# Chunked attention and a top-2 expert layer in one kernel: a new schedule for the attention, with its first loads, transposes and routing moved

## The chip, the cores and the metric

The kernel runs on one core of a Trainium2 chip. The number that counts is the device time of one execution in microseconds, the median of three runs. The core has five engines that each work through their own instructions in order: PE (matrix multiplications and transposes by matrix multiplication), DVE (vector), ACT (scalar and activation), POOL (GpSimd) and SP, which here only issues transfers. They wait for each other with semaphores. Transfers run on 16 DMA engines that all queues share. The profile is one execution recorded by the hardware.

## The reference

Two layers, the second fed by the first. The attention has 4 batches, 8 heads, 768 positions, head size 64. Positions are cut into chunks of 32; a chunk sees 16 positions before it, itself, 8 after it, and 8 memory rows.

```
scores = scale * q_c @ concat(mem_k, k_ctx).T
a      = softmax(scores)
out_c  = a @ concat(mem_v, v_ctx)
```

Its output, 3072 rows of 512, goes through a mixture of 8 experts (512 to 1024 to 512). Each row takes the two experts with the largest noisy gate values:

```
noisy  = x @ w_gate + log1p(exp(x @ w_noise)) * noise
top2   = the two largest, weights = softmax over the two
out    = sum over the two of  weight * (relu(x @ w1[e]) @ w2[e])
```

## The kernel before

**Attention.** A tile is 256 positions of one batch, so there are three tiles a batch and twelve in all, counted by `i`; `tp` is the tile within its batch. The main loop (L538) works on several tiles at once. In iteration `i` the scores of tile `i+1` are computed (`scores`: PE into PSUM, then a maximum and a subtraction on DVE), the exponentials of tile `i` are turned (`turn_p`: eight PE transposes, an ACT copy), `values` multiplies them with v and scales by the reciprocal sums, and tile `i-1` is sent to DRAM (`keep_x`, on SP, into `xd`), turned (`turn_x`: eight PE transposes and an ACT copy, L465 and L467) and multiplied with the gate weights (`gate`). `exps` is the exponential on ACT and comes near the end of the iteration.

**Input units.** k, q and v of a batch are loaded by POOL with a cast to bf16 (`load`, L112; 1.5 MB of fp32 each), into four buffers `nat`. Each is cut into three parts: a unit is one part. `mix` (L350) brings a part into an order in which it can be turned, `turn` (L366) transposes it with eight PE transposes into PSUM, `settle` (L375) copies it into `kT`, `qT` or `vT`, two copies for k and one for q and v. The nine units of a batch are spread over earlier iterations by `groups`. For batch 0 DVE does the first six mixes and shares the copies with ACT; after that POOL mixes and ACT copies.

**Spans of v.** `windows` turns `vT` back into rows for each chunk, 16 small PE transposes and one DVE copy (L386) for each half of a tile; `memory_rows` (L391) then adds the memory rows with two transfers from SP.

**Routing.** `Route` picks the two experts of the 768 rows of a batch, as a code for one of 28 pairs: noise on ACT, `choose` on DVE (the last step builds `ohp`, a 0/1 mask of rows by pairs, L255), `ranks` (place of a row within its pair, on PE), `weights` (L271 to L276), `place`, `total` (running counts, L293 and L297), `slots` (a one-hot of the rank, L303), `values` of the route (L308, POOL) and `lists` (L315, PE), which adds to `listed`, a table with the rows of each pair. Routing of a batch is spread over the iterations of the next one, by the `yield`s of `route`. The last batch is routed after the loop, in two portions.

**PSUM.** Most transposes share a ring of three buffers (`psT`); the gate's result shares one buffer with the sums of `values` (tag `ps_g`, L438 and L474).

**Experts.** Rows are gathered by pair from `xd` (`gathers`, POOL), the first six pairs by PE and the rest by DMA transposes on SP (L663), and worked through in 20 steps of one expert and two to four pairs. `load_expert` brings w1 and w2 of one expert with a cast, 2 MB as bf16, from POOL; experts 0, 1, 2 and 3 are loaded at the ends of iterations 3, 4, 6 and 8, expert 4 behind the second gathers, the others by `feed` during the steps. A pair is scattered to the output with `put` (L644, POOL) when its second expert is done; the pairs done in the last two steps are held in `held`.

**End.** If a pair has too many rows for the tables, a branch (L940) works on the rest; with this data it is not taken. The held scatters stand behind the branch in the text, but POOL's order is set by a scheduler there, which brings all but one of them ahead of it.

The order on PE, ACT, DVE and SP in the attention is written out by hand (`manual_schedule`). POOL's is set by a scheduler, with `pin` keeping mixes, loads, gathers and scatters in their order. The attention's buffers are cut from the end of `w_all`, the array of the expert weights (`scratch`), down into expert 3; experts 0 to 2 are free of them.

Of the kernel before, what the change touches and what calls it, by code (L numbers as in the profile page):

```python
# [22 lines left out]
def kernel(  # L23
# [82 lines left out]
    assert scol[0] // WE >= 3  # L106
    stage = xrow[1].rearrange("p s r -> p (s r)").bitcast(F32)

# [5 lines left out]
    for n in range(4):  # L114
        load(n)
# [14 lines left out]
    mks = stage[:, 0:2 * D].rearrange("p (x d) -> p x d", x=2)  # L130
    nc.sync.dma_start(out=mks, in_=mem_k.rearrange("b h m d -> (b h m) d").rearrange("(x p) d -> p x d", p=128))
    mkn = keep.tile([128, 2, D], BF16, name="mkn")
    nc.vector.tensor_copy(mkn, mks)
    mvs = stage[0:B * NM, 2 * D:2 * D + Dm].rearrange("p (h d) -> p h d", h=H)
    for b in range(B):
        nc.sync.dma_start(out=mvs[b * NM:(b + 1) * NM], in_=mem_v[b].rearrange("h m d -> m h d"))
    mvn = keep.tile([B * NM, Dm], BF16, name="mvn")
    nc.vector.tensor_copy(mvn.rearrange("m (c g d) -> m c g d", c=HP, g=2), mvs.rearrange("m (g c) d -> m c g d", g=2))
    wgs = stage[:, 2 * D + Dm:2 * D + Dm + KP * 2 * E].rearrange("p (k e) -> p k e", k=KP)
    nc.scalar.dma_start(out=wgs[:, :, 0:E], in_=moe_w_gate.rearrange("(kp p) e -> p kp e", p=128))  # L140
    nc.scalar.dma_start(out=wgs[:, :, E:2 * E], in_=moe_w_noise.rearrange("(kp p) e -> p kp e", p=128))
    wgn = const.tile([128, KP, 2 * E], BF16, name="wgn")
    nc.vector.tensor_copy(wgn, wgs)
# [46 lines left out]
    for i in range(2):  # L190
        nc.vector.memset(kT[i], 0.0)
    nc.vector.memset(vT[:, :, 0:LC], 0.0)
    nc.vector.memset(vT[:, :, LC + S:VP], 0.0)

# [12 lines left out]
    class Route:  # L207
# [23 lines left out]
        def choose(self):  # L231
# [23 lines left out]
            nc.vector.tensor_tensor(out=self.M, in0=pcode.unsqueeze(1).to_broadcast([128, n, NP]), in1=bc(pc[:, 0], NP), op=Alu.is_equal)  # L255
# [34 lines left out]

        def total(self):
# [8 lines left out]
        def slots(self, eng):  # L300
            n = self.n
            self.oh_l = work.tile([128, n, 128], BF16, name="oh_l")
            eng.tensor_tensor(out=self.oh_l, in0=bc(self.rr, 128), in1=io_l.unsqueeze(1).to_broadcast([128, n, 128]), op=Alu.is_equal)  # L303

# [18 lines left out]
    def route(b):  # L323
        r = Route(b * SO, SO, lgs[b])
        r.noise()
        yield
        advance(r.choose())
        yield
        r.ranks()
        r.weights(nc.vector)  # L330
        advance(r.place())
        advance(r.total())
        yield
        r.values(nc.gpsimd, 0, NV)
        r.slots(nc.vector)
# [3 lines left out]

    groups = [[(3 * b + x, part) for x, part in g] for b in range(B)
              for g in ([(0, 0), (0, 1), (1, 0)], [(0, 2), (1, 1), (1, 2)], [(2, 0), (2, 1), (2, 2)])]
# [11 lines left out]
    def mix_group(g):  # L355
        if g < 3 * B:
            for n, part in groups[g]:
                mix(n, part, nc.gpsimd)
            for n in ((), (g - 1, g), (g,))[g % 3]:
                load(n + 4)  # L360
# [627 lines left out]
```

## Time and profile before

| | us |
|---|---|
| median of three runs | 367.88 (366.38 to 369.55) |
| the profiled execution | 370.21 |
| its span, first to last instruction | 368.6 |
| PE busy | 289.4 (79%) |
| DVE busy | 175.4 (48%) |
| ACT busy | 144.9 (39%) |
| POOL busy | 131.6 (36%) |
| mean granted clock of PE | 0.913 |

The shares are averages over two stages: the attention and routing until about 154 us, and the experts after it. A row of the grouped lines has the line, engine and operation, what is written and read, the count, then busy time and mean ns of one, and the idle time of the engine just before with what ended it. A row of the timeline has start, length, engine, line and, in brackets, the idle time before it and what ended that. A row of the windows has the stretch, its length, the busy time of PE, weight loads, DVE, ACT and POOL, then the clock, the share of the DMA engines and GB/s. SPq and POOLq are the issuing sides of SP and POOL.

### The profile page before, as it was taken

How to read it: one execution, taken by the hardware profiler on the slowest of the kernel's cores; microseconds unless marked ns; L12 is line 12 of the kernel's file. 1: busy time of each engine (PE TensorE's matmuls, PEld its weight loads, DVE VectorE, ACT ScalarE, POOL GpSimd, SP SyncE). 2: the span in 40 equal slices, each digit the busy share in tenths (PEclk: the TensorE clock that was granted, in tenths of full speed). 3: DMA queues.
4: the chain of work that ended last, by engine and by line, in shares of the span. 5: the costliest groups of instructions: out<-in, count | busy, mean ns of one | idle time of the engine just before them, and what ended most of it. 6: DMA issues, size and time to landing. Idle time of an engine off the chain costs nothing.

```text
span 368.6 us, 8521 instructions
## 1 busy us (share of the span) xinstructions
PE 289.4 (79%) x3636; PEld 191.0 (52%) x3636; DVE 175.4 (48%) x408; ACT 144.9 (39%) x202; POOL 131.6 (36%) x173
## 2 busy tenths in 40 slices
PE   0476777667747451589999999999989999999970
PEld 0465667657646331465554445764436676555530
DVE  6963565896896978421133300974300233311330
ACT  1448768669843331034333144222234212334200
POOL 6279354453030023744275440162480032201131
PEclk9988788899898855599999999999999999999996
DMA  7999979997969020376999999821189982100020
GB/s 125 213 213 196 192 136 203 217 190 140 164 112 215 18 67 25 88 139 124 194 199 255 182 226 85 119 98 49 66 150 188 205 173 79 51 2 3 21 96 28
DMA packets 44156, 48.33 MB, mean 131 GB/s; under 512 B 19367, under 2 KB 33447, under 8 KB 44112
## 3 DMA queue, kind: packets, MB, share of 16 engines
q0 software_dynamic: 22672, 40.51, 57.5%
q1 hardware_dynamic: 17296, 7.08, 10.5%
q10 hardware_dynamic: 4144, 0.13, 0.8%
q8 instruction: 30, 0.49, 0.5%
q14 instruction: 14, 0.11, 0.1%
HBM read 64.88 MB, written 10.55 MB: 205 GB/s over the span
## 4 chain that ended last, share of the span: by engine, by line
PE 26%; issue 20%; DMA 6%; POOL 5%; DVE 5%; another core or an unknown queue 2%; POOLq 1%
PE p_y L690 12%; PE p_h L681 12%; DMA out_dram<-y,main_dst 5%; POOL out_dram L644 3%; POOL xt L638 2%; DVE w_all L455 1%; DMA xt<-xd,main_src 1%; DVE oh_l L303 1%; PE p_list L315 0%; PE p_xt L658 0%; POOL w_all L815 0%; POOLq L983 0%; DVE cum L297 0%; POOL w_all L816 0%
## 5 line engine op out<-in xcount | busy, mean ns | idle before, releaser
L681 PE MATMUL p_h<-xTt,w_all 128*128 128x256 bf16 (+3 forms) x672 | 102.9, 313 | 1.4 <-issue 1.0
L690 PE MATMUL p_y<-w_all,h 128*128 128x512 bf16 x448 | 100.1, 379 | 1.4 <-ACT y L694 1.4
L681 PEld LDWEIGHTS <-w_all 128*128 128x128 bf16 x672 | 65.9, 101 | 36.6 <-issue 2.0
L669 ACT ACTIVATE h<-p_h 128x512 bf16<-128x512 f32 (+1 forms) x79 | 43.4, 550 | 94.0 <-PE p_h L681 85.5
L690 PEld LDWEIGHTS <-h 128*128 128x128 bf16 x448 | 43.7, 98 | 51.7 <-issue 1.7
L644 POOL DMA_INDIRECT out_dram<-y,main_dst x28 | 31.0, 1108 | 105.9 <-DVE y L696 78.7
L667 DVE TENSOR_SCALAR h<-p_h 128x512 bf16<-128x512 f32 (+1 forms) x47 | 29.5, 630 | 80.6 <-PE p_h L681 66.7
L350 POOL COPY w_all<-w_all 128x1024 bf16<-128x1024 bf16 x30 | 30.5, 1043 | 27.3 <-PE p_t L366 21.8
L696 DVE SCALAR_TENSOR_TENSOR y<-p_y,main_w,y 128x512 f32<-128x512 f32 x28 | 21.0, 750 | 39.0 <-PE p_y L690 35.7
L638 POOL DMA_INDIRECT xt<-xd,main_src x28 | 27.2, 973 | 22.2 <-DMA xTt<-xt 8.8
L366 PE MATMUL p_t<-identb,w_all 128*128 128x128 bf16 x288 | 24.8, 243 | 13.2 <-DVE w_all L350 7.6
L694 ACT ACTIVATE y<-p_y,main_w 128x512 f32<-128x512 f32 x28 | 19.2, 688 | 38.2 <-PE p_y L690 34.8
L366 PEld LDWEIGHTS <-w_all 128*128 128x128 bf16 x288 | 20.4, 111 | 14.9 <-DVE w_all L350 8.0
L375 ACT COPY kT<-p_t 64x1024 bf16<-64x1024 bf16 x21 | 21.1, 1007 | 12.9 <-DVE kT L375 11.1
L383 PE MATMUL p_v<-identb,w_all 128*64 128x128 bf16 x384 | 18.5, 252 | 7.4 <-ACT w_all L375 4.8
L308 POOL TENSOR_TENSOR vals<-ohp,facts 128x1008 bf16<-128x1008 bf16 (+2 forms) x5 | 6.6, 1312 | 39.9 <-DVE facts L276 39.9
L433 ACT COPY pT<-p_p 128x1024 bf16<-128x1024 bf16 x12 | 12.1, 1010 | 20.1 <-PE p_p L430 20.1
L383 PEld LDWEIGHTS <-w_all 128*64 128x64 bf16 x384 | 14.7, 128 | 10.2 <-ACT w_all L375 5.4
L467 ACT COPY xT<-p_x 128x1024 bf16<-128x1024 bf16 x12 | 12.1, 1012 | 15.6 <-PE p_x L465 15.6
L455 DVE TENSOR_TENSOR w_all<-ps_o,rs 128x512 bf16<-128x512 f32 x24 | 15.5, 687 | 5.4 <-PE ps_o L447 3.1
L386 DVE COPY w_all<-p_v 128x1024 bf16<-128x1024 bf16 x24 | 16.0, 683 | 3.0 <-PE p_v L383 3.0
L418 DVE TENSOR_TENSOR sc<-ps_s,mx 128x1024 f32<-128x1024 f32 x12 | 14.7, 1225 | 4.1 <-ACT pb L423 3.3
(177 smaller groups left out, 283.2 us busy)
## 6 DMA issues: line engine op xcount, KB each, us to landing
w_all<-in_moe_w_dram POOLq DMA_DIRECT2D x16, 1024.0 KB
w_all<-in_moe_w_dram POOLq DMA_DIRECT2D x8, 512.0 KB
w_all<-in_k_dram POOLq DMA_DIRECT2D x4, 768.0 KB
w_all<-in_q_dram POOLq DMA_DIRECT2D x4, 768.0 KB
w_all<-in_v_dram POOLq DMA_DIRECT2D x4, 768.0 KB
xd<-w_all SPq DMA_DIRECT2D x12, 256.0 KB
w_all<-mvn SPq DMA_DIRECT2D x24, 32.0 KB
xt<-xd,main_src POOLq DMA_INDIRECT x28
```

Source lines behind the costliest of these rows:

```text
L350: i = eng.tensor_copy(home(n, part).rearrange("p s g d -> p g s d"), nat[n % 4].rearrange("p g (s d) -> p g s d", s=SP_)[:, :, part * 8:pa ...
L366: nc.tensor.transpose(out=p_t[:, s, :], in_=m[:, s].rearrange("p g d -> p (g d)"), identity=identb)
L375: (nc.scalar.copy if eng else nc.vector.tensor_copy)(to, src[rows])
L383: nc.tensor.transpose(out=p_v[j * 64:j * 64 + 64, i, c, :], in_=vT[:, c, c0 + j * 128:c0 + j * 128 + 64], identity=identb, tile_position=( ...
L638: i = nc.gpsimd.indirect_dma_start(out=xts[key].bitcast(I32), out_offset=None, in_=xd, in_offset=bass.IndirectOffsetOnAxis(ap=ix, axis=0))
L644: i = nc.gpsimd.indirect_dma_start(out=out if rows is None else rows, out_offset=bass.IndirectOffsetOnAxis(ap=ix, axis=0), in_=y, in_offse ...
L667: nc.vector.tensor_scalar(out=out_, in0=in_, scalar1=0.0, scalar2=None, op0=Alu.max)
L669: nc.scalar.activation(out=out_, in_=in_, func=Act.Relu)
L681: nc.tensor.matmul(out=o, lhsT=w(kp * F + f * 128, 128), rhs=x[:, kp], start=(kp == 0), stop=(kp == KP - 1))
L690: nc.tensor.matmul(out=p, lhsT=h[:, (f * n + j) * 128:(f * n + j + 1) * 128], rhs=w(KP * F + f * Dm, Dm), start=(f == 0), stop=(f == FB - 1))
L694: nc.scalar.activation(out=y, in_=p, func=Act.Copy, scale=weight)
L696: nc.vector.scalar_tensor_tensor(out=y, in0=p, scalar=weight, in1=y, op0=Alu.mult, op1=Alu.add)
```

## The change

- **First batch.** k, q and v of batch 0 are no longer loaded whole by POOL with a cast. Nine pieces, of 256 positions each, come as fp32 into the space of experts 0 to 2 (`early`), each in four transfers of 32 partitions, in the order in which they are used: k0 and k1 from SP, q0 from ACT, then v0, v1, q1, k2, v2, q2 from SP. `mix` converts them; DVE does the first three, POOL the others. The other loads follow behind on POOL: batch 1's k after the seventh mix, the next three after the ninth.
- **Units.** A group of units is now one tensor (k, q or v) of a batch from batch 1 on. Batch 0's nine are in the order of use. k of batch 1 is turned in iteration 1, q and v in iteration 2, batch 2's in 3 to 5, batch 3's in 6 to 8.
- **Iterations.** Tile 0 is worked through ahead of the loop, up to `values`. In the loop `exps(i+1)` stands ahead of `values(i)`; in the middle tile of a batch ACT copies the spans instead of DVE. `mvn`, `wgn`, `kT[1]` and the ends of `vT` are prepared later.
- **Rows turned by transfers.** `send_x` replaces `turn_x` for all tiles but the last two: two DMA transposes on SP, behind `keep_x`. The gate's PSUM tile moves to the ring `psT`.
- **Routing.** POOL builds the pair masks (six operations), the weights, the counts (`total_apart`) and the one-hots (`slots_apart`, six operations); DVE keeps `choose`, `place` and one weight column. The steps of a batch are spread more widely, `lists` of a batch at the end of its third iteration.
- **Experts.** 0, 1 and 2 load at the ends of iterations 7, 8 and 9, expert 3 between the first and the second gathers.
- **End.** POOL's order around the branch is written out by hand, so that the held scatters stand behind it.

```diff
+    early = wflat[:, 0:9 * 4 * 8 * D].bitcast(F32).rearrange("p (x a g c) -> p x a g c", x=3, a=3, g=2)
+    groups = [[(0, 0), (1, 0), (0, 1)], [(2, 0), (2, 1), (1, 1)], [(0, 2), (2, 2), (1, 2)]]
+    for b in range(1, B):
+        groups += [[(3 * b + x, part) for x, part in g]
+                   for g in [[(x, 0), (x, 1), (x, 2)] for x in range(3)]]
-    for n in range(4):
-        load(n)
+    def load_early(x, part, queue):
+        rows = (k, q, v)[x][0].rearrange("(g h) (a p s) d -> a h p g (s d)", g=2, a=3, s=8)[part]
+        for h in range(4):
+            queue.dma_start(out=early[h * 32:h * 32 + 32, x, part], in_=rows[h])
...
+            if apart:
+                for g in range(n):
+                    nc.gpsimd.tensor_scalar(out=self.M[:, g], in0=pcode, scalar1=pc[:, 0, g:g + 1], scalar2=None, op0=Alu.is_equal)
...
+        def total_apart(self, eng):
+            k = len(cum)
+            cum.append(const.tile([128, NP], BF16, name=f"cum{k}"))
+            h = self.n // 2
+            red = work.tile([128, h, NP], F32, name="redh")
+            eng.tensor_tensor(out=red, in0=self.M[:, 0:h], in1=self.M[:, h:2 * h], op=Alu.add)
+            for g in range(1, h):
+                eng.tensor_tensor(out=red[:, 0], in0=red[:, 0], in1=red[:, g], op=Alu.add)
+            eng.tensor_tensor(out=cum[k], in0=cum[k - 1], in1=red[:, 0], op=Alu.add)
...
+        def slots_apart(self, eng):
+            self.oh_l = work.tile([128, self.n, 128], BF16, name="oh_l")
+            for g in range(self.n):
+                eng.tensor_scalar(out=self.oh_l[:, g], in0=io_l, scalar1=self.rr[:, g:g + 1], scalar2=None, op0=Alu.is_equal)
...
         r.noise()
+        c = r.choose(True)
+        advance(c, 8)
         yield
-        advance(r.choose())
+        advance(c)
         yield
         r.ranks()
-        r.weights(nc.vector)
+        r.weights(nc.gpsimd)
+        r.values(nc.gpsimd, 0, NV)
+        r.total_apart(nc.gpsimd)
+        yield
         advance(r.place())
-        advance(r.total())
-        yield
-        r.values(nc.gpsimd, 0, NV)
-        r.slots(nc.vector)
+        r.slots_apart(nc.gpsimd)
         yield
         r.lists(0, NV)
...
+    def send_x(xr):
+        xT = work.tile([128, KP, 2, 128], BF16, name="xT")
+        for j in range(2):
+            nc.sync.dma_start_transpose(out=xT[:, :, j, :], in_=xr[:, j, 0:Dm])
+        return xT
...
-        ps_l = psG.tile([128, 2, 2 * E], F32, name="ps_l", tag="ps_g")
+        ps_l = psT.tile([128, 2, 2 * E], F32, name="ps_l", tag="ps_t")
...
+            if i + 1 < NT and i != 2:
                 sc = scores(i + 1)
+            if r and tp == 1:
+                next(r)
+            some(2 if tp == 2 else 1)
             pTs[i] = turn_p(pbs.pop(i))
+            if r and tp == 2:
+                next(r)
+            if tp < 2:
+                next_spans(0, nc.scalar if tp == 1 else None)
+            some(1)
+            keep_x(i - 1, nc.sync)
+            xTs_[i - 1] = (turn_x if i == NT - 1 else send_x)(xrs.pop(i - 1))
+            if tp < 2:
+                next_spans(1, nc.scalar if tp == 1 else None)
+            if i + 1 < NT and i != 2:
+                pbs[i + 1] = exps(sc)
             last = (lambda: gate(i - 1, xTs_.pop(i - 1))) if i == NT - 1 else None
             xrs[i] = values(i, pTs.pop(i), last)
+            some(4)
+            if i == 2:
+                mix_group(6)
+                sc = scores(i + 1)
+            if tp == 2:
+                next_spans(0)
+                next_spans(1)
+            if i == 2:
+                pbs[i + 1] = exps(sc)
             if i + 1 < NT:
+                gate(i - 1, xTs_.pop(i - 1))
...
+            if i in (7, 8, 9):
+                load_expert(i - 7)
...
     gathers(0, 0, 6)
+    load_expert(3)
     gathers(1, 0, 8)
...
+    with tc.manual_schedule(engines={ET.Pool}):
+        nov = nc.values_load(nxt[0:1, 0:1], min_val=0, max_val=NX + NP,
...
+        with tc.If(nov > 1):
...
+        for y, ix in held:
+            put(y, ix)
```

`some(n)` turns and settles the next n units of the iteration's group; `next_spans` is `windows` for tile `i+1` under its new name `spans`.

More of the change, by code (lines that the diff above doesn't have):

```diff
@@ L527, with unit @@
[L527 to L536 removed]
+        def unit(u, eng=nc.scalar):
+            settle(*u, turn(*u), eng)
+        for u in groups[0]:
+            mix(*u, nc.vector)
+            unit(u, nc.vector if u[0] == 1 else nc.scalar)
```

204 lines of the change are left out of this document (100 added, 104 removed).

## The prediction

> **What bounds the kernel now.** I read the head of the page first, then the grouped lines, then the order of time, then the chain of waits for the end.
>
> ```profile
> span 368.6 us, 8521 instructions
> 200.00:250.00 50.00, 50.00 (x297) 28.89 (x296) 20.84 (x46) 15.46 (x25) 17.95 (x16) 1.00 0.92 143
> 19.06 0.34 PE L401 MATMUL ps_s<-mkT,qT 128*128 128x16 bf16 x8 [1.65 <-DVE qT L375]
> 32.53 0.34 PE L440 MATMUL ps_g<-ones,pT 128*128 128x2 bf16 x8
> 62.09 0.34 PE L440 MATMUL ps_g<-ones,pT 128*128 128x2 bf16 x8
> 105.58 0.34 PE L440 MATMUL ps_g<-ones,pT 128*128 128x2 bf16 x8
> 134.68 0.39 PE L440 MATMUL ps_g<-ones,pT 128*128 128x2 bf16 x8
> ```
>
> There are two machines. From about 161 us the experts keep PE full (the windows row: 50.00 of 50.00 us at clock 1.00), so nothing there gets shorter unless PE work goes, and the change takes none away. Before that lies the attention, where no engine is full. The L440 rows are `values` of tiles 0, 3, 8 and 11: 102.2 us for eleven steps, 9.3 each. I keep score with these four marks.
>
> ```profile
> L416 DVE TENSOR_REDUCE mx<-ps_s 128x16 f32<-128x1024 f32 x12 | 14.7, 1225 | 3.3 <-PE ps_s L407 3.1
> L386 DVE COPY w_all<-p_v 128x1024 bf16<-128x1024 bf16 x24 | 16.0, 683 | 3.0 <-PE p_v L383 3.0
> L423 ACT ACTIVATE pb<-sc 128x1024 bf16<-128x1024 f32 x12 | 12.7, 1062 | 1.1 <-DVE sc L418 1.0
> L467 ACT COPY xT<-p_x 128x1024 bf16<-128x1024 bf16 x12 | 12.1, 1012 | 15.6 <-PE p_x L465 15.6
> L433 ACT COPY pT<-p_p 128x1024 bf16<-128x1024 bf16 x12 | 12.1, 1010 | 20.1 <-PE p_p L430 20.1
> L375 ACT COPY kT<-p_t 64x1024 bf16<-64x1024 bf16 x21 | 21.1, 1007 | 12.9 <-DVE kT L375 11.1
> L366 PE MATMUL p_t<-identb,w_all 128*128 128x128 bf16 x288 | 24.8, 243 | 13.2 <-DVE w_all L350 7.6
> PE ps_l L477 <- DVE rs L452: 8.7, 3, 4.6
> ```
>
> ACT waits 20.1 us for `p_p` and 15.6 for `p_x`: it stands idle because PE, in order, is stuck elsewhere. What sticks it is a late exponential (queued on ACT behind k copies of 2 us a unit), the gate's PSUM tile, which shares one buffer with `ps_g` (8.7 us in three waits), and DVE.
>
> **Start.** Nine fp32 pieces replace the first k, q, v.
>
> ```profile
> 10.38 1.01 DVE L350 COPY w_all<-w_all 128x1024 bf16<-128x1024 bf16 x3
> 6.58 0.16 POOL L168 IOTA pab<- 128x1 f32 x1
> L138 DVE CAST mvn<-w_all 32x512 bf16<-32x512 f32 x1 | 0.4, 414 | 0.9 <-DMA w_all<-in_mem_v_dram 0.9
> L375 DVE COPY qT<-p_t 128x1024 bf16<-128x1024 bf16 x2 | 2.4, 1219 | 0.0
> 350.00:369.00 19.00, 7.18 (x34) 3.04 (x31) 3.00 (x4) 0.69 (x1) 4.51 (x5) 0.83 0.17 60
> ```
>
> The last window holds little but 2 KB fp32 scatter rows: 60 GB/s at 0.17 of 16 engines gives 2048 B / 60 GB/s x 0.17 = 5.8 ns a row. [...] A mix from fp32 is new: 0.34 (a third of 1.01) to 1.2 (the PSUM copy), and I take 0.8, twice the 512-column cast. Then k0 7.3 to 8.1, q0 to 8.9, the q copy 9.7 to 10.9, k1 to 11.7, PE 0.7 (24.8 us over 36 units), two ACT copies 2.0: scores(0) at 14.5 instead of 19.06, **-4.5**. The wait on mem_v (0.9) moves behind them.
>
> [...]
>
> **Batch 0 and the packed second batch.** Next are v0, two span groups, exp, `turn_p`; memory rows land some 3 us after their copy (estimate, half of what they take under load below); values(0) at about 25.5 against 32.53, -7.0. Part of it is given back: the nine units of batch 1 (twelve ACT copies, 12.1 us) sit in iterations 1 and 2, where before they began ahead of values(0). ACT after values(0): v2 copied at 28.4, exp to 30.8, q2 31.8; two k units, pT and two spans copies to 40.8, exp 41.9, third k unit 44; three q and pT to 48, three v to 51.8; scores(3) behind them, exp to 55.3; k unit, pT 59.3, k unit; values(3) at 60.5 instead of 62.09: **-1.6** in all. The kT[1] memset, which DVE now does here, lies under ACT's copies.
>
> **Iterations 3 to 8.** Per batch ACT has 12 unit copies, 3 exps, 3 pT and, new, 2 span copies (12.1 + 3.2 + 3.0 + 2.0, about 21 us with the noise functions); its 3 xT copies go. DVE loses two span copies (1.4) and the mask, weight, sum and one-hot work.
>
> ```profile
> L303 DVE TENSOR_TENSOR oh_l<-rank,io_l 128x768 bf16<-128x768 f32 (+2 forms) x5 | 3.9, 789 | 0.0
> L308 POOL TENSOR_TENSOR vals<-ohp,facts 128x1008 bf16<-128x1008 bf16 (+2 forms) x5 | 6.6, 1312 | 39.9 <-DVE facts L276 39.9
> L350 POOL COPY w_all<-w_all 128x1024 bf16<-128x1024 bf16 x30 | 30.5, 1043 | 27.3 <-PE p_t L366 21.8
> L273 POOL CAST facts<-d 128x4 bf16<-128x4 f32 (+1 forms) x6 | 1.2, 196 | 0.4
> ```
>
> With exps ahead of `values`, `turn_p` no longer waits for them, and ACT sets the pace. I laid out one batch with three shared PSUM buffers, from the start of its first scores, ACT's ends being: k 3.8, pT 4.8, k 6.9, exp 8.0, k 10.0, noise 10.5; q 11.5, pT 12.5, span 13.5, q 14.5, span 15.5, exp 16.6, q 17.6; v 18.6, v 19.6, pT 20.6, v 21.6, exp 22.7, and the next scores at 23.7. `values` begins at 5.6, 13.2 and 20.6. I add 1 a batch for hand-overs. From values(3) to values(8) that makes 38.7 + 1.5 (a batch and a half) = 40.2 instead of 43.5: **-3.3**. POOL has nine mixes (9.4), vals (1.9) and 22 small operations between 0.2 (the cast) and 0.5 (0.2 and 128 columns at the pace of vals), at most 11: below 24, and masks and one-hots are due half an iteration later. If POOL is late, the rank or list matmul holds PE.
>
> **Last three tiles.** They have no units, so short steps and every wait counts.
>
> ```profile
> 128.89 0.08 DVE d L271
> 133.01 1.02 PE p_list L315 x6
> 109.89 1.48 SPq L391 DMA_DIRECT2D w_all<-mvn  x2
> 111.43 0.43 SPq L484 DMA_DIRECT2D xd<-w_all  x1
> 117.32 0.67 PE L447 MATMUL ps_o<-w_all,pT 64*32 64x64 bf16 x63 [0.16 <-DMA w_all<-mvn]
> 159.76 0.83 POOL L76 DMA_DIRECT2D w_all<-in_moe_w_dram  x1
> 158.56 2.60 SPq L663 DMA_TRANSPOSE xTt<-xt  x2
> 162.42 1.01 POOL L638 DMA_INDIRECT xt<-xd,main_src  x1 [1.83 <-DMA xTt<-xt]
> 170.09 0.95 POOL L638 DMA_INDIRECT xt<-xd,main_src  x1 [6.66 <-DMA xTt<-xt]
> ```
>
> Routing of batch 2 held DVE and PE from 128.89 to 134.03; now it is spread and its list follows values(11). The gate has PSUM of its own. Without new waits values(9) follows values(8) by 6.2 us (tail of its iteration, scores, `turn_p`, pT), values(10) by 4.2, values(11) by 4.9 (max, subtract, exp, `turn_p`, pT): 15.3 us instead of 29.1. New wait: `xT` comes from two transposes on SP, 1.3 us each, behind keep_x (0.43); behind them on SP stand the memory rows of the next tile, for which `values` waits, and PE's gate holds the next scores. A transpose with DMA quiet was done within 3.9 us of its start (158.56 to 162.42), one with an expert coming in about 9 (a buffer came free at 170.09); the memory rows under load took 6 us (111.37 to 117.32). Experts 0 to 2 now load just here. A tile's transposes run while PE waits for those of the one before, and from a gate to the xr of two tiles on it is about 5 us, so with a latency L from xr the period is (L + 5)/2: at L = 5.4 (0.43, 2.6 and 2.4 to land) there is almost no wait, at 12 it is 8.3 against 5. That is 0 to 3.3 a tile for three tiles, and up to 7 for memory rows: 0 to 17, and I take 7, with both kinds loaded about half the time: 22.3 us, **-6.8**. In the iterations with units xr ends 7.3 after the gate and the limit is (L + 7.3)/2, below their 7.9 until L = 8.5: covered, and 1.7 a tile if all were loaded. The list behind costs **+0.7**.
>
> **Experts.** Expert 3 now loads between the first gathers and the second ones.
>
> ```profile
> GB/s 125 213 213 196 192 136 203 217 190 140 164 112 215 18 67 25 88 139 124 194 199 255 182 226 85 119 98 49 66 150 188 205 173 79 51 2 3 21 96 28
> 174.94 1.56 SPq L663 DMA_TRANSPOSE xTt<-xt  x1
> 194.59 6.91 PE p_h L681 x32
> ```
>
> At some 200 GB/s (the busy slices) its 2 MB take about 10 us; it is used at step 3, some 30 us in. Block 1's transposes ended at 176.5 and step 4 uses them at 194.59: 10 us later still fits. **0**, or up to 10 if not.
>
> **End.** Scatters went out ahead of the branch, which waits until they have landed; one more comes behind it.
>
> ```profile
> 356.57 0.98 POOL L644 DMA_INDIRECT out_dram<-y,main_dst  x1 [0.80 <-DVE y L696]
> 357.22 0.75 DVE L696 SCALAR_TENSOR_TENSOR y<-p_y,main_w,y 128x512 f32<-128x512 f32 x1 [0.92 <-PE p_y L690]
> 361.27 0.11 POOLq L940
> 362.27 0.98 POOL L644 DMA_INDIRECT out_dram<-y,main_dst  x1 [4.72 <-DMA out_dram<-y,dst]
> ```
>
> y is done at 357.97, yet the last scatter starts at 362.27. Behind the branch it starts 0.3 after y, 358.25: **-4.0**. The branch then waits only for scatters of earlier steps, long landed. If the branch waited for other engines too, the gain would be gone: 0 to -4.0.
>
> **Sum.** -1.6 - 3.3 - 6.8 + 0.7 - 4.0 = -15.0 (the -4.5 is inside the -1.6). The profiled execution took 370.21, its span 368.6; its 355.2 at the median's ratio (367.88 / 370.21) gives **353**.
>
> **Rivals.**
> - [...] Chance 0.10.
> - The steps don't get shorter: PE with its three buffers, not ACT, is the pace (13.2 us of waits ahead of the p_t transposes stand for it, ACT's 35.7 against), and the last three gain only what the transposes cost. Left are -1.6 and -4.0, with 0 to 7 of stalls: 362 to 369. Chance 0.16.
> - Expert 3 delays block 1's tiles: 10 us on PE at step 4, 358 to 363. The 18 us of slack speak against. Chance 0.06.
> - Slower: every transpose is late. Period (L + 7.3)/2 over eleven steps from 25.5 equals the old 134.7 plus 3.3 (4.0 of the end less 0.7) at L = 13.2. For: SP is in order, keep_x is ahead, the GB/s row stays near 200 until 80 us. At L = 15 it is 25.5 + 122.7 = 148.2, +13.5 - 3.3, 378; at 14, 373. Above the 9 to 12 seen under load, so 0.10.
>
> **Chances.** The forecast has 0.58, between 346 (no stall) and 363 (17 of stall). Range 344 to 367, 2 lower for a cheaper start: it leaves out the slower case, the upper end of the second rival and a little below. About 1% is what a measurement tells: faster below 364.2, slower above 371.6. Faster: 0.58 + 0.10 + 0.05 + 0.05 = 0.78; same: 0.11 + 0.01 and a little of the slower case, 0.13; slower 0.09.
>
> **What would show it.** First scores near 14.5; `values` near 25.5, 60.5, 99 and 122; ACT's idle ahead of pT gone from 20.1 to below 10; gate waits on the DMA of xT of 5 to 10 us in all, in the last tiles; the last scatter 0.3 us after y. Wrong would be: xT waits in every iteration, rank matmuls waiting for POOL, or PE gaps after the first expert.

## The result, and the profile after

The kernel became slower: 400.73 us (median of four runs, 396.86 to 405.56) against 367.13 of the kernel before in the same runs; ratio 1.082 (95% interval 1.072 to 1.093). Forecast were 353 us, and 344 to 367. Two of the four runs (402.86 and 405.56) were slow ones at a lower clock (0.861 and 0.864, against 0.870 and 0.876), and the ratio compares the other two with the kernel before. The profiled execution took 398.6 us, its span is 396.8.

Lines of the page after: span, load per slice, two of the queues, and three groups.

```profile
span 396.8 us, 8486 instructions
...
GB/s 201 209 170 143 221 159 95 167 109 64 61 63 107 205 192 185 164 29 32 144 229 174 159 216 236 202 166 166 99 44 158 167 205 196 48 49 4 20 45 72
...
q0 software_dynamic: 21856, 38.15, 51.6%
q1 hardware_dynamic: 31520, 13.87, 21.8%
...
L521 PE MATMUL ps_l<-wgn,xT 128*128 128x16 bf16 x96 | 5.2, 175 | 37.1 <-DMA xT<-w_all 36.0
...
L471 ACT COPY pT<-p_p 128x1024 bf16<-128x1024 bf16 x12 | 12.2, 1017 | 16.3 <-PE p_p L468 16.3
...
L485 PE MATMUL ps_o<-w_all,pT 64*32 64x64 bf16 x768 | 9.4, 216 | 12.0 <-DMA w_all<-mvn 12.0
```

The new line is L521, the gate: PE stood idle 36.0 us ahead of it for the transposed rows. L485, `values`, waited another 12.0 us for memory rows; in the kernel before it was 1.3 us. (Most of these 12.0 are not the transposes' doing: see the first experiment.) Where this happened stands in the order of time on PE (L439 the first scores, L478 the start of `values`, L485 its main part, L521 the gate).

```profile
12.44 0.41 PE L439 MATMUL ps_s<-mkT,qT 128*128 128x16 bf16 x8
24.86 0.40 PE L478 MATMUL ps_g<-ones,pT 128*128 128x2 bf16 x8
29.77 0.94 PE L485 MATMUL ps_o<-w_all,pT 64*32 64x64 bf16 x64 [4.52 <-DMA w_all<-mvn]
...
59.65 0.28 PE L521 MATMUL ps_l<-wgn,xT 128*128 128x16 bf16 x4 [11.56 <-DMA xT<-w_all]
62.54 0.27 PE L521 MATMUL ps_l<-wgn,xT 128*128 128x16 bf16 x4 [2.61 <-DMA xT<-w_all]
...
79.47 0.35 PE L478 MATMUL ps_g<-ones,pT 128*128 128x2 bf16 x8
...
128.28 0.35 PE L478 MATMUL ps_g<-ones,pT 128*128 128x2 bf16 x8 [0.32 <-ACT pT L471]
...
147.58 0.27 PE L521 MATMUL ps_l<-wgn,xT 128*128 128x16 bf16 x4 [7.94 <-DMA xT<-w_all]
151.32 0.28 PE L521 MATMUL ps_l<-wgn,xT 128*128 128x16 bf16 x4 [3.47 <-DMA xT<-w_all]
...
161.61 0.28 PE L521 MATMUL ps_l<-wgn,xT 128*128 128x16 bf16 x4 [5.15 <-DMA xT<-w_all]
166.28 0.27 PE L521 MATMUL ps_l<-wgn,xT 128*128 128x16 bf16 x4 [4.39 <-DMA xT<-w_all]
169.16 0.37 PE L478 MATMUL ps_g<-ones,pT 128*128 128x2 bf16 x8 [0.25 <-ACT pT L471]
```

Three gates hold nearly all of it: tile 0 (14.2 us in its two halves), tile 8 (11.4) and tile 9 (9.5). The other seven sent tiles cost next to nothing. The issuing side of SP shows when those tiles' transfers were sent; tile 5's stands among them for comparison, and so does tile 1's.

```profile
40.93 6.01 SPq L511 DMA_TRANSPOSE xT<-w_all  x2
...
50.46 9.82 SPq L511 DMA_TRANSPOSE xT<-w_all  x2
...
105.37 2.56 SPq L511 DMA_TRANSPOSE xT<-w_all  x2
...
133.93 4.82 SPq L511 DMA_TRANSPOSE xT<-w_all  x2
...
142.25 9.66 SPq L511 DMA_TRANSPOSE xT<-w_all  x2
```

From the start of a pair's issue to the gate's second half it took 62.54 - 40.93 = 21.6 us (tile 0), 151.32 - 133.93 = 17.4 (tile 8) and 166.28 - 142.25 = 24.0 (tile 9). Even the issue grew, from 2.56 us a pair to 9.82. These are the stretches in which the loads run: inputs of the next batches, issued from 20 to 49 us and busy until about 64, and experts 0 to 2, six loads issued from 124 to 134 us and busy until about 168. Tile 1's pair was sent into such a stretch too, but its gate came late enough, at 72.8 us, not to wait.

Two rows of the windows: one in the first stall, one for the stretch from `values` of tile 3 to that of tile 8.

```profile
52.00:56.00 4.00, 0.00 (x0) 0.00 (x0) 0.00 (x0) 0.00 (x0) 0.00 (x0) 0.50 1.21 142
79.50:128.30 48.80, 33.62 (x919) 28.94 (x918) 31.14 (x76) 34.23 (x40) 27.77 (x54) 0.83 0.53 79
```

From 52 to 56 us PE, DVE, ACT and POOL all stand still while the DMA engines are full. Where the 28.2 us of span come from, by the start of `values`:

| stretch | before | after | difference |
|---|---|---|---|
| start to tile 3 | 62.09 | 79.47 | +17.4 |
| tile 3 to 8 | 43.5 | 48.8 | +5.3 |
| tile 8 to 11 | 29.1 | 40.9 | +11.8 |
| tile 11 to the first gather | 13.3 | 14.8 | +1.5 |
| experts to the last y (first gather included) | 210.0 | 205.6 | -4.4 |
| last y to the end | 10.6 | 7.3 | -3.4 |

### The profile page after: what moved, and what is told of

It reads as the page before. It is cut to its first block, busy times and chain, and to the rows that moved or that the text cites. A ratio compares the mean times of both kernels' runs of the same rounds, so it can differ in the third digit from the quotient of the medians.

```text
span 396.8 us, 8486 instructions
## 1 busy us (share of the span) xinstructions
PE 293.0 (74%) x3556; PEld 191.0 (48%) x3556; DVE 158.5 (40%) x364; ACT 146.2 (37%) x203; POOL 155.8 (39%) x239
## 3 DMA queue, kind: packets, MB, share of 16 engines
q1 hardware_dynamic: 31520, 13.87, 21.8%
## 4 chain that ended last, share of the span: by engine, by line
PE 31%; DMA 16%; issue 10%; POOL 6%; DVE 4%; SPq 3%; ACT 2%; POOLq 1%; DVEq 0%
PE p_h L742 16%; PE p_y L751 12%; DMA out_dram<-y,main_dst 10%; DMA xT<-w_all 5%; SPq L511 2%; POOL out_dram L705 2%; POOL oh_l L334 2%; DMA xTt<-xt 1%; ACT kT L410 1%; DMA xt<-xd,main_src 1%; POOL xt L699 1%; PE p_t L397 1%; SPq L429 1%; PE p_v L418 1%; POOL ohp L269 0%
## 5 line engine op out<-in xcount | busy, mean ns | idle before, releaser
L742 PE MATMUL p_h<-xTt,w_all 128*128 128x256 bf16 (+3 forms) x672 | 101.6, 310 | 0.0
L742 PEld LDWEIGHTS <-w_all 128*128 128x128 bf16 x672 | 65.0, 99 | 34.8 <-issue 0.2
L730 ACT ACTIVATE h<-p_h 128x512 bf16<-128x512 f32 (+1 forms) x79 | 43.5, 551 | 90.9 <-PE p_h L742 80.0
L705 POOL DMA_INDIRECT out_dram<-y,main_dst x28 | 31.1, 1110 | 83.2 <-DVE y L757 68.2
L382 POOL COPY w_all<-w_all 128x1024 bf16<-128x1024 bf16 x27 | 27.4, 1041 | 29.8 <-PE p_t L397 29.0
L397 PE MATMUL p_t<-identb,w_all 128*128 128x128 bf16 x288 | 31.0, 279 | 10.7 <-ACT kT L410 2.6
L757 DVE SCALAR_TENSOR_TENSOR y<-p_y,main_w,y 128x512 f32<-128x512 f32 x28 | 21.0, 750 | 39.0 <-PE p_y L751 38.4
L521 PE MATMUL ps_l<-wgn,xT 128*128 128x16 bf16 x96 | 5.2, 175 | 37.1 <-DMA xT<-w_all 36.0
L397 PEld LDWEIGHTS <-w_all 128*128 128x128 bf16 x288 | 25.0, 128 | 14.0 <-issue 8.0
L410 ACT COPY kT<-p_t 64x1024 bf16<-64x1024 bf16 x24 | 24.2, 1008 | 17.4 <-PE p_t L397 17.2
L521 PEld LDWEIGHTS <-xT 128*128 128x128 bf16 x96 | 3.9, 103 | 38.9 <-DMA xT<-w_all 37.2
L493 DVE TENSOR_TENSOR w_all<-ps_o,rs 128x512 bf16<-128x512 f32 x24 | 15.5, 686 | 15.4 <-PE ps_o L485 15.0
L471 ACT COPY pT<-p_p 128x1024 bf16<-128x1024 bf16 x12 | 12.2, 1017 | 16.3 <-PE p_p L468 16.3
L485 PE MATMUL ps_o<-w_all,pT 64*32 64x64 bf16 x768 | 9.4, 216 | 12.0 <-DMA w_all<-mvn 12.0
L410 ACT COPY w_all<-p_t 128x1024 bf16<-128x1024 bf16 x12 | 11.8, 1020 | 16.2 <-PE p_t L397 16.2
```

The costliest lines, as they stand in the source:

```text
L382: i = eng.tensor_copy(home(n, part).rearrange("p s g d -> p g s d"), rows)
L397: nc.tensor.transpose(out=p_t[:, s, :], in_=m[:, s].rearrange("p g d -> p (g d)"), identity=identb)
L410: (nc.scalar.copy if eng is nc.scalar else eng.tensor_copy)(to, src[rows])
L705: i = nc.gpsimd.indirect_dma_start(out=out if rows is None else rows, out_offset=bass.IndirectOffsetOnAxis(ap=ix, axis=0), in_=y, in_offse ...
L730: nc.scalar.activation(out=out_, in_=in_, func=Act.Relu)
L742: nc.tensor.matmul(out=o, lhsT=w(kp * F + f * 128, 128), rhs=x[:, kp], start=(kp == 0), stop=(kp == KP - 1))
```

## The experiments

The theory after the result: transposes by transfer are late where loads run beside them, PE waits for them in order, and that is nearly the whole loss. Rivals: the transfers cost wherever they are sent; the routing on GpSimd or the new order costs; the memory rows are the cause. The kernel before took 371 to 372 us in the runs of the first twelve kernels and 367.2 in those of the last four, so ratios are compared.

### The transfers out, and moved

```diff
-            xTs_[i - 1] = (turn_x if i == NT - 1 else send_x)(xrs.pop(i - 1))
+            xTs_[i - 1] = turn_x(xrs.pop(i - 1))
```

> The changed kernel, but all rows are turned by PE and copied by ACT again, so that SP carries no transposes in the attention. Theory A (the transfers' latency under DMA load is the loss): of the 36 us in which PE waits for xT nothing is left, some 5 come back as PE and ACT work, the last values starts near 139 instead of 169 us, and the time is about 370 (362 to 378). Theory B (the new order of the loads is the loss, whoever turns the rows): the waits for the memory rows stay at 10 us or grow, and the time stays above 385. Theory C (the routing on GpSimd sets the pace): the waits move to the masks and one-hots, time above 385.

Measured: 373.97 us, ratio 1.007 (1.004 to 1.010). By the ratios 7.5 of the 8.2% are gone. The waits for memory rows stay at 9.9 us, as theory B had it, but the time falls in spite of them: most of them (7.5 us, tiles 0 to 2) came with the new front, and not with the transposes. What is left is slower than before although the new end is in it; the routing experiment below takes that up. In this kernel `values` starts at 25.4, 43.5, 53.1, 65.9, 74.8, 85.8, 94.6, 104.2, 114.2, 123.7, 131.9 and 139.6 for tiles 0 to 11; after had 66.6 for tile 2 and 155.4 and 169.2 for tiles 10 and 11, and kept its distance of 12 to 15 us in between. So the pairs sent in quiet stretches cost nothing, and three sent in loaded ones cost nearly all.

```diff
-            if i in (7, 8, 9):
-                load_expert(i - 7)
...
     gathers(0, 0, 6)
-    load_expert(3)
+    for e in range(4):
+        load_expert(e)
```

> The changed kernel, with the loads of experts 0 to 2 taken from the ends of iterations 7 to 9 and put behind the first gathers, ahead of expert 3. If the transposes are late only under load: the xT waits of the last tiles (about 21 us) fall below 5, the one of iteration 2 (14 us, under input loads) stays, and the first expert starts 8 to 12 us late: about 388 to 392. If a transpose is slow by itself: the waits of the last tiles stay above 15 us and the time is 405 or more.

Measured: 429.63 us in a single run, far from both. In the attention the first theory holds: the gates of the last tiles wait 1.4 us in all, and the stretch from tile 8 to 11 takes 22.2 us instead of 40.9, while the gate of tile 0, still beside input loads, waits 20.2. But then the expert stage stalls. Two rows of its waits (total, times, longest):

```profile
PE p_h L740 <- DVE h L726: 14.3, 1, 14.3
PE p_h L740 <- DMA w_all<-in_moe_w_dram: 8.9, 3, 5.9
```

In the second PE waits for weights. In the first it waits for `h` from DVE, which itself stood 16.0 us for a table that GpSimd delivered late, behind its gathers and loads. The loads can't simply go behind the attention: the first expert matmul came 15.7 us after the first gather instead of 4.6, and the stage from there to the last y grew from 201.0 to 232.6 us. I had not priced that.

The other way round, the transfers alone in the kernel before:

```diff
+    def send_x(xr):
+        xT = work.tile([128, KP, 2, 128], BF16, name="xT")
+        for j in range(2):
+            nc.sync.dma_start_transpose(out=xT[:, :, j, :], in_=xr[:, j, 0:Dm])
+        return xT
...
-                xTs_[i - 1] = turn_x(xrs.pop(i - 1))
+                xTs_[i - 1] = (turn_x if i == NT - 1 else send_x)(xrs.pop(i - 1))
```

> The kernel before, with one part of the change alone: the rows of tiles 0 to 9 turned by two DMA transposes each on SP. Theory A: the loads of the kernel before are spread over the same time, so L is about 9 to 14 us in most iterations and the gate waits 10 to 25 us in all: 377 to 392. Theory B: no more than 1% from the kernel before.

Measured: 444.05 us, ratio 1.196 (1.189 to 1.203), far above what was expected. Rows of its order of time, SP's issues and the gate (L483), and of its windows:

```profile
94.40 1.45 SPq L391 DMA_DIRECT2D w_all<-mvn  x2
96.45 3.12 SPq L473 DMA_TRANSPOSE xT<-w_all  x2
102.04 0.27 PE L483 MATMUL ps_l<-wgn,xT 128*128 128x16 bf16 x4 [11.54 <-DMA xT<-w_all]
...
113.17 2.55 SPq L473 DMA_TRANSPOSE xT<-w_all  x2
116.33 0.28 PE L483 MATMUL ps_l<-wgn,xT 128*128 128x16 bf16 x4 [6.05 <-DMA xT<-w_all]
117.10 0.28 PE L483 MATMUL ps_l<-wgn,xT 128*128 128x16 bf16 x4 [0.50 <-DMA xT<-w_all]
...
126.02 4.33 SPq L473 DMA_TRANSPOSE xT<-w_all  x2
136.59 0.59 PE L483 MATMUL ps_l<-wgn,xT 128*128 128x16 bf16 x8 [11.37 <-DMA xT<-w_all]
...
136.60:138.00 1.40, 1.36 (x21) 1.27 (x22) 0.19 (x1) 0.00 (x0) 0.00 (x0) 0.50 0.00 0
```

Two things add up, and every gate waits, 89.0 us in all. In this kernel's order on SP the memory rows of tile i+1 stand ahead of the transfer of tile i-1, and they wait for span copies on VectorE; some 28 of the 89 us lie ahead of a pair's issue. The rest lies between issue and landing. A pair is short when it runs alone: 113.17 to 116.33 for the first half, 3.9 us for both, the figure that the prediction had for quiet DMA. Beside the two loads of one expert (issued at 120.20 and 121.00, the pair at 126.02) it took 10.6 us, and the two other pairs sent 5 to 7 us behind an expert's loads took 11.0 and 9.3. All three landed just as the traffic beside them stopped; the last row shows 0 GB/s right after 136.59.

```diff
-            xTs_[i - 1] = (turn_x if i == NT - 1 else send_x)(xrs.pop(i - 1))
+            xTs_[i - 1] = (send_x if 2 <= i - 1 <= 7 else turn_x)(xrs.pop(i - 1))
```

> After with the transfers kept for tiles 2 to 7 alone, which the changed kernel sent while few loads ran; tiles 0, 1, 8 and 9, sent beside input or expert loads, go back to TensorE. If the loads beside them are what makes the transfers late, these six are in time and take six 1.03 us evictions off ScalarE: 2 to 5 us under the 374 of the kernel with all of them on TensorE, 369 to 372. If a transfer is late wherever it is sent, or ScalarE doesn't set the pace, 374 to 380.

Measured: 371.33 us, ratio 0.998 (0.995 to 1.001), against 1.007 with all rows on TensorE. The quiet transfers are a small gain, 0.9% by the ratios, as expected if loads are what makes a pair late.

### Are the loads the cause? The loads moved onto the transfers

Both kernels load experts 0 to 2 in iterations 4, 5 and 6; the first sends tiles 2 to 7, the second none.

```diff
-            if i in (7, 8, 9):
-                load_expert(i - 7)
+            if i in (4, 5, 6):
+                load_expert(i - 4)
```

> Transfers for tiles 2 to 7 alone, and experts 0 to 2 loaded in iterations 4, 5 and 6, beside those transfers, instead of 7, 8 and 9. Read against the next kernel, which has the same loads and all rows on TensorE. If it is loads beside them that make transfers late, this kernel loses 8 us or more to it, where without the loads the six transfers won 2.6. If they are late for their place in the program and not for the loads, it stays within -4 to +2 us of it.

> All rows on TensorE, experts 0 to 2 loaded in iterations 4, 5 and 6: the control for the kernel above. Loads in iterations 3, 4, 6 and 8 gave 381; with the first one later and the fourth still behind the first gathers, 373 to 382 by either theory.

Measured: 382.17 us, ratio 1.041 (1.035 to 1.047), with the transfers, and 368.52, 1.005 (1.001 to 1.008), without, which is better than the 373 to 382 expected of it. The same six transfers that won 0.9% without loads lose 3.6% beside them. Tile 5 without and with the load, for each kernel SP's issue and the gate's second half, then the stretch in the windows (last numbers: clock, DMA share, GB/s). First the six transfers without loads:

```profile
91.73 2.52 SPq L511 DMA_TRANSPOSE xT<-w_all  x2
97.36 0.26 PE L521 MATMUL ps_l<-wgn,xT 128*128 128x16 bf16 x4 [1.47 <-DMA xT<-w_all]
```

```profile
88.00:98.00 10.00, 6.43 (x214) 5.57 (x217) 7.02 (x13) 6.85 (x7) 7.49 (x9) 0.99 0.39 77
```

And with expert loads beside them, tiles 5 and 6:

```profile
90.75 2.90 SPq L511 DMA_TRANSPOSE xT<-w_all  x2
99.64 7.31 SPq L511 DMA_TRANSPOSE xT<-w_all  x2
108.25 0.28 PE L521 MATMUL ps_l<-wgn,xT 128*128 128x16 bf16 x4 [4.16 <-DMA xT<-w_all]
122.75 0.27 PE L521 MATMUL ps_l<-wgn,xT 128*128 128x16 bf16 x4 [4.15 <-DMA xT<-w_all]
```

```profile
98.00:108.00 10.00, 0.55 (x9) 0.28 (x6) 1.10 (x2) 3.20 (x4) 1.78 (x2) 0.59 1.30 173
```

5.6 us at 77 GB/s; 17.5 and 23.1 at 170 to 200 GB/s, beside six loads issued from 80 to 96 us. Neither the six transfers nor these loads cost anything alone (0.998 and 1.005, against 1.007 without both); beside each other they lose 3.6%. So the loads beside the transfers are shown to be the cause.

### Do the transfers cost only those who wait for them?

All rows are turned on TensorE, and for tiles 0 to 7 the transfers are issued as well, into columns that nobody reads.

```diff
+            if i < 9:
+                send_x(xrs[i - 1], xU[:, i % 2])
+            xTs_[i - 1] = turn_x(xrs.pop(i - 1))
```

> All rows turned on TensorE, and for tiles 0 to 7 the two transfers are issued too, into columns that nobody reads. If the transfers cost by the wait for them alone, 373 to 377. If they cost by holding up SyncE's queue and the other transfers (memory rows, input loads), a third or more of the 27 us is back: 382 and over.

Measured: 388.24 us, ratio 1.043 (1.038 to 1.049): by the ratios 13 us over the kernel without them, though no gate waits. Its order of time, SP and PE:

```profile
40.71 5.93 SPq L512 DMA_TRANSPOSE w_all<-w_all  x2
46.75 2.23 SPq L429 DMA_DIRECT2D w_all<-mvn  x2
...
68.49 0.21 PE L485 MATMUL ps_o<-w_all,pT 64*32 64x64 bf16 x1 [15.39 <-DMA w_all<-mvn]
```

The memory rows of tile 2, issued right behind the transfers, landed over 21 us later; with none ahead of them (issued at 46.77, last wait over at 54.05) they took 7.3 us at most. Is that their place in the queue, or a load on everything? The transfers were moved behind the memory rows:

```diff
-            if i < 9:
-                send_x(xrs[i - 1], xU[:, i % 2])
...
                 next_spans(1)
+            if i < 9:
+                send_x(xr, xU[:, i % 2])
```

> As the kernel with unused transfers for tiles 0 to 7 (388.2), with each pair of transfers issued behind the next tile's memory rows instead of ahead of them; nothing reads the transferred columns. If the transfers cost there by standing ahead of the memory rows in one queue, most of the 14 us is back: 374 to 379. If they slow every transfer beside them wherever they stand, 384 to 390.

Measured: 386.38 us, ratio 1.040 (1.036 to 1.044), as if the place didn't matter. But GpSimd waited 17.1 us there with expert 2's second load, for the last unused transfer into columns of that expert; that is the experiment's own doing. Without the last of them (`i < 8`):

> Unused transfers behind the memory rows, for tiles 0 to 6 alone, so that the load of expert 2, which waited 17 us for the last of them, no longer does. Read by tile 7's start: 104.2 us without transfers, 120.3 with them ahead of the memory rows, 111.3 behind. If that 7 us is the transfers' own share of the engines, it stays at 110 to 113 and the time falls to 379 to 383; if it was the place alone, the start comes to 104 to 107 and the time to 374 to 378.

Measured: 378.20 us, ratio 1.029 (1.024 to 1.034, two runs); `values` of tile 7 starts at 111.2 us, against 104.2 without transfers and 120.3 with them ahead. The start is where the first theory had it, the time at the border of the two. So some 9 of the 16 us at that point are the place in the queue, and 7 remain. They still sit in the memory rows, now tile 3's, which come behind tile 0's transfers in the queue; a row of that kernel's PE:

```profile
72.89 0.21 PE L485 MATMUL ps_o<-w_all,pT 64*32 64x64 bf16 x1 [4.79 <-DMA w_all<-mvn]
```

How far the rest is a share of the engines, and how far still order within the queue, these runs don't separate.

### What else the change cost

Routing back on VectorE, all rows on TensorE:

```diff
-        c = r.choose(True)
+        c = r.choose()
...
-        r.weights(nc.gpsimd)
+        r.weights(nc.vector)
         r.values(nc.gpsimd, 0, NV)
-        r.total_apart(nc.gpsimd)
...
+        advance(r.total())
-        r.slots_apart(nc.gpsimd)
+        r.slots(nc.vector)
```

> All rows turned on TensorE, and one-hots, pair masks, weights and totals back on VectorE as before. The kernel with rows on TensorE showed TensorE idle 9.4 us for the pair masks of GpSimd (three batches). If that wait is on the path, 5 to 9 us come back: 365 to 369. If it lies in slack that another engine fills, 372 to 377.

Measured: 369.39 us, ratio 0.997 (0.993 to 1.001): 1.0% gained, about 4 us, just below the gain expected. It comes mostly in the last tiles (21.9 us from tile 8 to 11 instead of 25.4); from tile 3 to 8 nothing changes (48.5 and 48.3). The rank matmuls' waits for the pair masks fell from 12.3 us (9.4 of them for GpSimd's) to 7.1 between 50 and 155 us.

```diff
-            if i in (7, 8, 9):
-                load_expert(i - 7)
+            if i in (3, 4, 6, 8):
+                load_expert((3, 4, 6, 8).index(i))
...
     gathers(0, 0, 6)
-    load_expert(3)
```

> All rows turned on TensorE, and experts loaded where the kernel before loads them (iterations 3, 4, 6 and 8). In the kernel with rows on TensorE the chain has a 6.96 us memory-row transfer at 118.5 us, beside expert loads. If the late expert loads cost it that, 366 to 370. If the loads only change which memory rows they hold up, 373 to 378.

Measured: 381.04 us, ratio 1.021 (1.012 to 1.029), worse than either theory had it. The trace shows where: expert 0's loads, issued at 58.95 and 59.71, meet the transfer of the routing's noise values, which ACT had issued at 48.04 and DVE needs:

```profile
78.97 0.21 DVE L246 TENSOR_TENSOR nl<-ns,nz 128x48 f32<-128x48 f32 x1 [9.33 <-DMA nz<-in_moe_noise_dram]
```

With no expert load there the same step stood at 71.31 and did not wait for the transfer. GpSimd's pair masks follow it, and PE stood idle 10.97 us for them; `values` of tile 5 starts at 93.8 us instead of 85.8. That the loads delay the noise values is read from the two traces, not tried.

### Looking for a version that beats both

The two edits above together, `send_x` for tiles 2 to 7 and routing on VectorE, and then the front as well:

> After with both repairs at once: transfers for tiles 2 to 7 alone, and routing back on VectorE. Alone, against the 374.0 of all rows on TensorE, they gave 2.6 and 4.6 us. If they act on different waits they add, 366 to 368; if both only uncover the next wait (memory rows, GpSimd's copies), 368.5 to 371.

Measured: 369.16 us, ratio 0.993 (0.990 to 0.996). They add only in part: 0.3% below the routing alone, which the intervals don't tell apart.

```diff
     load_early(2, 0, nc.sync)
-    load_early(2, 1, nc.sync)
-    load_early(1, 1, nc.sync)
-    load_early(0, 2, nc.sync)
     for b in range(B):
         nc.sync.dma_start(out=mvs[b * NM:(b + 1) * NM], in_=mem_v[b].rearrange("h m d -> m h d"))
+    load_early(2, 1, nc.sync)
+    load_early(1, 1, nc.sync)
+    load_early(0, 2, nc.sync)
...
         spans(0, 0, 1)
+        load_early(1, 2, nc.sync)
```

> The same, and memory rows of tile 0 ahead of the pieces of the last unit but one: the memory values are loaded behind the seventh piece group, the rows queued before the last piece group and the gate weights. The kernel with routing on VectorE showed TensorE idle 3.85 us for these rows in tile 0 and 1.5 and 1.3 in tile 1. If the front still sets tile 3's start, 1 to 3 us below the kernel without it, 364 to 367; if the packing of batch 1's units on ScalarE in iterations 1 and 2 takes it back, no difference within 1 us.

Measured: 370.52 us, ratio 0.997 (0.994 to 0.999). No gain; `values` of tile 3 came 1.4 us earlier and that of tile 4 2.6 us later, with 3.0 us of new waits ahead of the gate of tile 2, whose pair took 10.3 us there.

The end alone, in the kernel before, and again with more runs:

```diff
+    with tc.manual_schedule(engines={ET.Pool}):
...
+        for y, ix in held:
+            put(y, ix)
```

> The kernel before, with the end of the change alone (the order around the branch written out, held scatters behind it). The prediction's term: the last scatter starts 0.3 us after its y instead of 4.3, 4 us less: 363 (ratio 0.987 to 0.992). Rival: the end hangs on something else and the ratio is 1.00.

> Before with the new end alone, once more and with more runs, beside the others: 0.989 (0.982 to 0.996) the first time. If the last scatter's 4 us is all of it, 0.987 to 0.991; nothing else in the kernel differs.

Measured: 367.13 us, ratio 0.989 (0.982 to 0.996), and 364.57, ratio 0.991 (0.988 to 0.994). And with the gate's sums moved to `psT` besides:

```diff
-        ps_l = psG.tile([128, 2, 2 * E], F32, name="ps_l", tag="ps_g")
+        ps_l = psT.tile([128, 2, 2 * E], F32, name="ps_l", tag="ps_t")
```

> Before with the new end (0.989 of before) and the gate's sums in the transposes' PSUM buffers, the part of the change that takes the wait of TensorE on the row sums' reciprocal away (8.7 us in three tiles of the trace of before). If those waits are on the path, 4 to 8 us more than the end alone: ratio 0.968 to 0.979, 359 to 363. If TensorE then waits for VectorE in the next step anyway, ratio 0.985 to 0.992. A loss (over 0.995) would mean that a transposes' buffer held by the gate stops the next transposes.

Measured: 369.53 us, ratio 0.994 (0.991 to 0.997): the 8.7 us of waits go, and nothing is won. One of its waits, in the stretch from 100 to 140 us in which the 8.7 lay, says where PE stops instead:

```profile
PE p_list L315 <- DVE oh_l L303: 7.4, 2, 4.7
```

That wait was 3.7 us before. Another 4.4 us, ahead of the rank matmuls for DVE's span copies, are new, and tile 3 to 8 takes 47.3 us instead of 43.5: with the gate's sums in the transposes' buffers that stretch is longer.

Of the versions that beat both kernels the kernel before with the new end is the simplest. At 0.991 it can't be told apart from the best of the others (0.993), which has the new end too; so the rest of the change, repaired, has won nothing that these runs show.

## Why the prediction was wrong, point by point

- **Last three tiles (-6.8).** The step that failed, here and in the next point: it took 9 us for a loaded transpose and 12 as the worst, from the expert stage's rows, where the loads are fed in parts; measured are 17.4 and 24.0 us here, and 17.5 and 23.1 with loads put on purpose. The stretch took 40.9 us, not 22.3; with rows on TensorE 15.5 of the 18.6 us too many go. The row behind the 9 us could not show more: one load of 1 MB was issued beside it, at 159.76, and the buffer came free at 170.09, as the traffic fell (before, last number GB/s):

```profile
164.00:168.00 4.00, 4.00 (x25) 2.25 (x24) 0.92 (x3) 1.67 (x3) 0.00 (x0) 1.00 1.13 206
168.00:172.00 4.00, 4.00 (x24) 2.15 (x23) 0.93 (x2) 1.47 (x3) 1.61 (x2) 1.00 0.48 104
```

  The pairs beside one expert's loads, 9.3 to 11.0 us, ended with the traffic as well. Beside six queued loads the GB/s were no higher (174 to 200) and a pair took about twice as long. So the price goes with how much is queued beside a pair and not with the GB/s; this is read from the traces, as no run varies the number of loads alone. The 15.3 us without waits were too short as well: with the expert loads behind the attention the stretch took 22.2 with 1.4 of gate waits (close to the 22.3 by chance, as 7 of those were waits), with rows on TensorE 25.4, with routing on VectorE besides 21.9.
- **"Covered" in the iterations with units.** The formula asked for L below 8.5 us and allowed 1.7 us a tile beyond it. It assumed quiet transfers there. No run shows the 2.4 to land in its L of 5.4: alone, a pair was done 1.4 us after the end of its issue (113.17 + 2.55, and 117.10). Tile 0's, sent into the queued input loads, took 21.6 us, and the gate lost 14.2; tile 3 started at 79.47, not 60.5, and with rows on TensorE 13.6 of these 19.0 us go. Memory rows I had put at 6 us under load; behind the transposes that nobody reads they took over 21. In the quiet iterations the term held: 0.9 us of waits from tile 3 to 8.
- **The slower rival.** Its mechanism came true, with another shape: it wanted every transpose late by L = 13.2, and what came was three tiles late by far more. Its 0.10 was too little for a price bounded only by rows of another stage. It also named the stage that decided, DMA near 200 GB/s until 80 us.
- **Why beside loads?** By the page's packets (q1, after against 20640 in the kernel with rows on TensorE) a transpose is (31520 - 20640) / 20 = 544 packets of (13.87 - 11.25) / 20 = 0.131 MB in all. At the 182 GB/s measured beside two loads a pair's bytes would take 1.4 us (an estimate from these rows), so its size alone doesn't make it late. The runs agree in that a pair is late only while another queue is busy: 3.9 us alone, 9.3 to 11.0 beside two loads, 17.4 to 24.0 in after's three stalls. What happens there between the queues none of them shows. The queue's row (packets, MB, share) of the page of the kernel with rows on TensorE:

```profile
q1 hardware_dynamic: 20640, 11.25, 16.7%
```

- **Start (-4.5).** Forecast were 14.5, by way of k1's copies: the part of the scores that needs them started at 14.76, the first part at 12.44; right, and mixes from fp32 took 0.69 on DVE. The sum's 7.3, at which DVE starts on k0, needs k0 landed by then, and no run shows a time to land from which that follows; k0's mix began at 6.60 and q0's at 7.90, after 0.59 and 0.61 us of waiting for the piece. And the nine pieces didn't come at the pace of the scatter rows, at whose 5.8 ns their 2304 rows are 13.4 us. The last mix, a row of GpSimd's order of time, after:

```profile
29.84 1.04 POOL L382 CAST w_all<-w_all 128x1024 bf16<-128x1024 f32 x1 [5.83 <-DMA w_all<-in_q_dram]
```

  It waited until 29.84. At the 201 GB/s of the first slice nine pieces of 512 KB are 23.5 us. Whole loads ran at 213 GB/s before; SP issued the last piece only by 22.34 us; and from 20.27 batch 1's k loads beside it. What each of these adds, no run separates. I had scaled from scatter rows of another direction; the first 0.10 of my chances stood for slower pieces, at 354 to 357.
- **Batch 0 and the packed second batch (-1.6).** `values` of tile 0 started at 24.86 (25.5 forecast) but its main part at 29.77, for the memory rows. With rows on TensorE tile 3 still came at 65.9, 3.8 later than before. On the way lie 7.5 us of waits for the memory rows of tiles 0 to 2, which before had none; how much the packing and the late pieces add isn't separated.
- **Iterations 3 to 8 (-3.3).** Wrong by 8.6 us: 48.8 instead of 40.2, and 48.3 with rows on TensorE. I had ACT as the pace with 1 us a batch of hand-overs; the window above has it busy 34.23 of 48.80, and its idle time ahead of `pT`, which should fall below 10 us, is 16.3. The second rival, that the steps don't get shorter, was right here in what came; its reason, PE as the pace, isn't shown, as PE is busy only 33.62. A row of PE's waits in that stretch, after:

```profile
PE p_rank L277 <- POOL ohp L269: 6.0, 2, 3.2
```

  Masks "due half an iteration later" were in fact late, but these 6 us aren't the reason: with routing on VectorE the stretch still took 48.5. Which part of the new order lengthens it stays open; the gate's sums in the transposes' buffers, which alone took the kernel before from 43.5 to 47.3 there, are a candidate.
- **List (+0.7), experts (0).** +1.5 and -4.4. From its first matmul to the last y the expert stage took 201.0 us here and 205.3 before; in the two runs of before with the new end, whose code is that of before up to there, it took 205.3 and 202.2. So I read little into the -4.4; the delay of block 1 did not come.
- **End (-4.0).** Right. After's last scatter (L705) and the y ahead of it (L757):

```profile
388.79 0.75 DVE L757 SCALAR_TENSOR_TENSOR y<-p_y,main_w,y 128x512 f32<-128x512 f32 x1 [0.92 <-PE p_y L751]
389.82 0.98 POOL L705 DMA_INDIRECT out_dram<-y,main_dst  x1 [0.69 <-DVE y L757]
```

  The scatter starts 0.28 us after y; alone the end is worth 0.9 to 1.1%, 3 to 4 us.

## What to carry to other kernels

A transfer that replaced an engine's work had the latency of the DMA stage in which it ran, here 3.9 us a pair alone and 17.4 to 24.0 beside queued loads: take its price from a row with the same loads beside it, in the same queue, and see whether that row ended only because its loads did. Where no such row exists let the range reach to several times the loaded one. PE, which works in order, stood idle 35 us for three late pairs, and small transfers queued behind a pair paid too (memory rows, 21.7 us instead of 7.3). A wait that goes (8.7 us here) is worth nothing until it is known what comes next.

## What the runs showed of the hardware that was not expected

- Two transposes of 128x512 bf16 within SBUF took 3.9 us from the start of their issue where DMA had been quiet (7 GB/s in the ten us before), 5.6 us at 77 GB/s, 9.3 to 11.0 us beside two expert loads (182 to 191 GB/s), and 17.4 to 27.5 us beside more queued loads (146 to 200 GB/s; the 27.5 is tile 0's pair in the kernel with the experts behind). Their issue on SP, 1.3 us each, took up to 8.26 us.
- Transposes that nobody waits for cost 13 us: memory rows of 32 KB that stood behind them in SP's queue landed after 21.7 us instead of 7.3.
- GpSimd took 0.58 us for a 128x128 one-hot in bf16 and 0.33 us for a 128x28 mask.
